# MLP units regrouped into ten blocks of 128 and one of 96 in a two-layer decode step

## The chip, the cores and the metric

The kernel runs on one core of a Trainium2 chip. The metric is the device time of one execution in microseconds; a version's time is the median over its runs. The engines that matter here are TensorE (PE, with its weight loads shown apart as PEld), VectorE (DVE), ScalarE (ACT), GpSimd (POOL), and SyncE (SP), whose queue issues every data transfer. The transfers run on 16 DMA engines.

## What is computed

One token (a row x of 512 numbers) passes through attention A, MLP B, attention A, MLP B, each with a layer norm before it and a residual sum after it. Both layers use the same weights and the same cache.

```python
# A: 32 heads of 128, cache of 4096 keys
q = layernorm(x) @ wq                       # 512 -> 32 x 128
p = softmax((q . k_cache) * 128 ** -0.5)    # per head, over 4096 keys
x = x + (p . v_cache) @ wo                  # 32 x 128 -> 512
# B: 1376 units
h = gelu(layernorm(x) @ w1 + b1)            # 512 -> 1376
x = x + h @ w2 + b2                         # 1376 -> 512
```

Everything is 32-bit floating point. The key and value caches hold 32 x 4096 x 128 numbers each, so that a layer reads far more than it computes.

## The kernel before

The heads are taken in eight groups of four (`G`); layer 0 goes through the groups upwards and layer 1 downwards, so that the last group's caches, and part of the group before it, need not be read twice. For each group `scores` (L230) multiplies the query with the keys, `softmax` follows, and the values are summed either on TensorE (`values`, L260) or on VectorE and ScalarE (`weighted`, L271, `weighted_by_act`, L265). All weights and caches come into one large tile, `arena`, by transfers that `load` (L85) issues on SP's queue in an order written out by hand. A transfer that overwrites a place waits on SP's queue for the last reader of that place, and all later transfers queue behind it.

The MLP (`mlp`, L335) has 1376 hidden units. Before the change they are split in four runs of `FJ` = 344 units, one for each quadrant of 32 partitions, and each run is cut into eleven pieces (`FB`) of 32. Block c, the c-th piece of each of the four runs, so holds 4 x 32 = 128 units, except that the last piece of each run has only 24. The host fills the last block of w2 with zero rows, so that w2 is 128 partitions x 11 x 512 numbers, 256 KB for each block.

`hidden(i)` (L349) computes the units of the blocks in `HIDDEN[i]`, (0 to 3), (4 to 7), (8 to 10), with four products side by side for each quarter of the input, each for one quadrant of 32 output partitions: 128 columns each, and 88 each for the last three blocks. `turned(i)` (L364) transposes the result on VectorE, `gelu` (L370) applies the scale, bias and activation, and the loop from L409 multiplies each block's 128 values with the 128 partitions of its piece of w2 (L414), four products for a block, one for each quarter of the 512 outputs. In the profile each of those 32-bit products shows as two records. All 44 products add into `pM`.

`W2_PARTS` (L47) cuts the transfers of w2: blocks 0-3, 4-5, 6-7, 8-9 and 10 in layer 0, and 0-3, 4-7, 8-9 and 10 in layer 1. Block 10 is a transfer of its own in both layers. In layer 0 there is room for eight blocks (`W2_AT`), so the transfers of blocks 8-9 and of block 10 are issued, through `follow` (L622), after the products of block 3; block 10 goes where block 2 was. In layer 1 they are the last two transfers into the core, and the products of blocks 8 to 10, a sum at L640 and the store of the output at L641 end the kernel.

Of the kernel before, what the change touches and what calls it, by code (L numbers as in the profile page):

```python
# [17 lines left out]
P = 128  # L18
D = 512
H, S, DH = 32, 4096, 128  # L20
F = 1376
G = 8
J = 4
C = 8
FJ = F // J
FB = 11
EPS = 1e-5
U = 512
KEPT = 6

NC = 4 * U
# [3 lines left out]
SPARE = 2 * BLOCK + STAY  # L35
# [4 lines left out]
AHEAD = 64  # L40
X_AT, B1_AT, B2_AT = 0, 8, 8 + FB
K2_HOME = 12 * NC

V1_HOME = *(2 * BLOCK + NC * c for c in range(5)), 8 * NC, 6 * NC, 7 * NC
W2_AT = tuple(SPARE + U * (c % 8) for c in range(FB)), tuple(U * c for c in range(FB))
PITCH = 1024
W2_PARTS = ((0, 4), (4, 6), (6, 8), (8, 10), (10, FB)), ((0, 4), (4, 8), (8, 10), (10, FB))  # L47
HIDDEN = ((0, 4), (4, 8), (8, FB))
W1_AT = (0, 4 * J * 32 * 4, 4 * J * 32 * 8)
# [11 lines left out]
def decode_layers(ctx: ExitStack, tc: tile.TileContext, k, v, w, w1, w2, out):  # L61
    nc = tc.nc
# [20 lines left out]
    arena = const.tile([P, ARENA], F32, name="arena")  # L83

    def load(at, src):  # L85
        t = arena[:, at : at + src.shape[-1]]
        tc.keep_in_program_order(nc.sync.dma_start(t, src))  # L87
        return t

    def pin(ins):  # L90
        tc.keep_in_program_order(ins)

    def chunk(t, i=0):
        return t[:, NC * i : NC * (i + 1)].rearrange("p (j n) -> p j n", j=4)
# [31 lines left out]

    fixed = small("fixed", 2 * FB + 7)
    b1c, colsum, b2c = fixed[:, :FB], fixed[:, FB : 2 * FB], fixed[:, 2 * FB : 2 * FB + 4]
# [20 lines left out]
    pM, pN = pO[:, 2 * P : 3 * P], pO[:, 3 * P :]  # L149
# [185 lines left out]
    def mlp(xs, s, w1_t, w2_t, xb, rows, fill, follow):  # L335
        hs, rstd = pH[layer], []
        if fill is None:
            nm, ss, _ = mean_of(xs, s, pN[:, 0:1], True)
            nm_s, nmr, cb, late = small("nm_s"), small("negm"), colsum, HIDDEN[0][1]
            nc.vector.tensor_copy(nm_s, nm)  # L340
        else:
            centred = small("xs", 8).rearrange("p (c i) -> p c i", i=2)
            nc.gpsimd.memset(centred[:, :, 1], 1.0)
            _, ss, _ = mean_of(xs, s, pN[:, 0:1], True, centred[:, :, 0])
        nc.gpsimd.tensor_tensor(xb, xs[:, :, 0], b2c, op=ALU.add)
        if fill is not None:
            xs = centred

        def hidden(i):  # L349
            at, first = hs[i], W1_AT[i]  # L350
            n = min(32 * HIDDEN[i][1], FJ) - 32 * HIDDEN[i][0]
            for c in range(4):
                for j in range(J):
                    f = first + n * (J * c + j)
                    pin(nc.tensor.matmul(at[32 * j : 32 * j + 2, :n], xs[:, c, :], w1_t[:, f : f + n],
                                         start=(c == 0), stop=(c == 3)))
                if i == 0 and c == VAR_AT:
                    rstd.append(rstd_of(ss, pN[:, 1:2], True))
                if i == 0 and c == VAR_AT and fill is None:
                    nc.gpsimd.tensor_tensor(nmr, nm_s, rstd[0], op=ALU.mult)  # L360
                    nc.gpsimd.tensor_scalar(cb[:, late:], colsum[:, late:], nmr, None, op0=ALU.mult)
                    nc.gpsimd.tensor_tensor(cb[:, late:], cb[:, late:], b1c[:, late:], op=ALU.add)

        def turned(i):  # L364
            ht = work.tile([P, 32 * 4], F32, name="pt")
            n = HIDDEN[i][1] - HIDDEN[i][0]
            pin(nc.vector.transpose(ht[:, : 32 * n], hs[i][:, : 32 * n]))  # L367
            return ht

        def gelu(i, ht):  # L370
            b0, b1_ = HIDDEN[i]
            n = b1_ - b0
            h, u, g = (small("gelu_" + k, FB)[:, b0:b1_] for k in "hug")
            if fill is not None:
                pin(nc.vector.scalar_tensor_tensor(u, of_32(ht, n), rstd[0], b1c[:, b0:b1_], op0=ALU.mult, op1=ALU.add))  # L375
                nc.gpsimd.tensor_copy(colsum[:, b0:b1_], of_32(ht, n, 1))
            elif i > 0:
                pin(nc.vector.scalar_tensor_tensor(u, of_32(ht, n), rstd[0], cb[:, b0:b1_], op0=ALU.mult, op1=ALU.add))
            else:
                pin(nc.vector.scalar_tensor_tensor(h, of_32(ht, n, 1), nm_s, of_32(ht, n), op0=ALU.mult, op1=ALU.add))  # L380
                pin(nc.vector.scalar_tensor_tensor(u, h, rstd[0], b1c[:, b0:b1_], op0=ALU.mult, op1=ALU.add))
            nc.scalar.activation(g, u, AF.Gelu_apprx_tanh)  # L382
            if fill is not None and b1_ == FB:
                nc.scalar.activation(small("m"), g[:, :1], AF.Exp, scale=0.0)
            return g

        if fill is not None:
            idle(fill, pS, 2 * P)
        hidden(0)
        if fill is None:  # L390
            hidden(1)
            pin(nc.vector.transpose(rows[:, P : 2 * P], rows[:, :P]))
        ht = turned(0)
        if fill is None:
            hidden(2)
        else:
            idle(fill, pO, 2 * P)
            idle(fill, pO, 2 * P)
        for i, (b0, b1_) in enumerate(HIDDEN):
            if i == 1 and fill is not None:  # L400
                for n in (512, 256):
                    idle(fill, pS, n)
                hidden(1)
                ht = turned(1)
                idle(fill, pS, 2 * P)
            g = gelu(i, ht)
            if fill is None and b1_ < FB:
                ht = turned(i + 1)
            for c in range(b0, b1_):  # L409
                if c == b0 + 2 and i == 1 and fill is not None:  # L410
                    hidden(2)
                    ht = turned(2)
                for j in range(J):
                    pin(nc.tensor.matmul(pM[32 * j : 32 * j + 1, :], g[:, c - b0 : c - b0 + 1],  # L414
                                         w2_t[c][:, P * j : P * (j + 1)], start=(c == 0), stop=(c == FB - 1)))
                for at, src in follow.get(c, ()):
                    load(at, src)
            if i == 1 and fill is not None:
                idle(fill, pS, 2 * P)
# [15 lines left out]
    w2_t = [[arena[:, at : at + U] for at in homes] for homes in W2_AT]  # L435
# [4 lines left out]
    for layer in range(2):  # L440
# [23 lines left out]
        for n, g in enumerate(order):  # L464
            first, final = n == 0, n == G - 1
# [55 lines left out]
            elif final:  # L521
# [9 lines left out]
                for a, b in END_PARTS[layer]:  # L531
                    at = BLOCK - NC + U * a
# [20 lines left out]
            if layer == 1 and n == 0:  # L553
                wo_t = chunk(arena[:, PAIR : PAIR + NC])
            elif final:
                at = PAIR + NC * layer
                for a, b in WO_PARTS[layer]:
                    load(at + U * a, of_w(wo_at(g), 1)[:, U * a : U * b])
                wo_t = chunk(arena[:, at : at + NC])
                if layer == 0:  # L560
                    load(HELD, w1[:, : W1_AT[1]])
                for a, b in W2_PARTS[layer][: 1 if layer == 0 else 4]:
                    load(W2_AT[layer][a], w2[:, U * a : U * b])
                if layer == 0:
                    load(HELD + W1_AT[1], w1[:, W1_AT[1] : W1_AT[2]])
            else:
                t = load(PAIR, of_w(wo_at(g) if layer == 0 else wq_at(g - 1), 2))
                wo_t, wq_next = (chunk(t, i) for i in ((0, 1) if layer == 0 else (1, 0)))
# [17 lines left out]
            if final:  # L586
                if layer == 0:
                    row_to_quadrants(row)
                    for a, b in W2_PARTS[0][1:3]:
                        load(W2_AT[0][a], w2[:, U * a : U * b])  # L590
                        if a == 4:
                            load(HELD + W1_AT[2], w1[:, W1_AT[2] :])
                idle(last_v, pO, 256)
# [15 lines left out]
        at = work.tile([P, P], F32, name="pt")  # L609
# [9 lines left out]
        if layer == 0:  # L619
            first_k, next_wq = part(k, G - 2, 0, 1), of_w(wq_at(G - 2), 1)  # L620
            follow = {
                3: (*((W2_AT[0][a], w2[:, U * a : U * b]) for a, b in W2_PARTS[0][3:]),  # L622
                    (SPARE + NC - U, first_k[:, NC - U :])),
                5: ((SPARE + NC, next_wq[:, : 2 * U]),),
                7: ((SPARE + NC + 2 * U, next_wq[:, 2 * U :]),),
                9: ((SPARE, first_k[:, : 2 * U]),),
            }
        mlp(x1, s1, w1_t, w2_t[layer], xb, *((None, last_v) if layer == 0 else (ends, None)), follow)
        if layer == 0:
# [4 lines left out]
            g = G - 2  # L634
# [9 lines left out]
def columns(a):  # L644

    return np.ascontiguousarray(a.reshape(J, 4, 32, -1).transpose(0, 2, 1, 3).reshape(P, 4, -1))
# [41 lines left out]
```

## Time and profile before

| | us |
|---|---|
| median of the three runs | 675.82 |
| the three runs | 673.79, 675.82, 676.31 |
| the profiled execution | 673.33 |
| span in its profile (first to last instruction) | 671.6 |
| around the span | 1.7 |

The profile is of one execution. Its span is what the views below divide up; the 1.7 us around it belong to the execution's time and to no instruction. Times in the views are counted from the span's start. A transfer "lands" when its last part is there; the name on the right of an arrow is what is read, on the left what is written.

### The profile page before, as it was taken

How to read it: one execution, taken by the hardware profiler on the slowest of the kernel's cores; microseconds unless marked ns; L12 is line 12 of the kernel's file. 1: busy time of each engine (PE TensorE's matmuls, PEld its weight loads, DVE VectorE, ACT ScalarE, POOL GpSimd, SP SyncE). 2: the span in 40 equal slices, each digit the busy share in tenths (PEclk: the TensorE clock that was granted, in tenths of full speed). 3: DMA queues.
4: the chain of work that ended last, by engine and by line, in shares of the span. 5: the costliest groups of instructions: out<-in, count | busy, mean ns of one | idle time of the engine just before them, and what ended most of it. 6: DMA issues, size and time to landing. Idle time of an engine off the chain costs nothing.

```text
span 671.6 us, 6013 instructions
## 1 busy us (share of the span) xinstructions
PE 299.7 (45%) x2236; PEld 79.7 (12%) x2236; DVE 407.1 (61%) x510; ACT 215.4 (32%) x697; POOL 5.2 (1%) x26
## 2 busy tenths in 40 slices
PE   1511703415116053165768986704316025065597
PEld 1000100101001010011114311101001001011124
DVE  3059679498696886971322313288597694973513
ACT  0047074190560823802011200083290650910010
POOL 1000000000000000000000000000000000000000
PEclk9965755757558557578689998655757559557799
DMA  9999999999999999999999999999999999999997
GB/s 377 437 437 438 435 437 437 403 461 437 437 437 397 444 426 434 433 429 426 425 415 399 422 422 438 437 433 433 431 433 437 437 430 402 462 426 414 431 414 286
DMA packets 11556, 285.29 MB, mean 425 GB/s; under 512 B 1284, under 2 KB 1288, under 8 KB 3720
## 3 DMA queue, kind: packets, MB, share of 16 engines
q1 hardware_dynamic: 11528, 284.92, 99.1%
q8 instruction: 17, 0.28, 0.2%
q14 instruction: 11, 0.09, 0.0%
HBM read 284.92 MB, written 0.00 MB: 424 GB/s over the span
## 4 chain that ended last, share of the span: by engine, by line
DMA 64%; PE 17%; DVE 15%; issue 1%; another core or an unknown queue 1%; SPq 1%; ACT 0%; DVEq 0%; ACTq 0%
DMA arena<-in_v 37%; DMA arena<-in_k 24%; PE pS L232 8%; DVE arena L274 7%; PE pO L262 5%; DMA arena<-in_w 4%; DVE arena L279 3%; DVE arena L311 2%; PE pO L283 1%; DVE arena L287 1%; DVE arena L215 1%; SPq L87 1%; PE pB L323 1%; DVE arena L309 0%
## 5 line engine op out<-in xcount | busy, mean ns | idle before, releaser
L269 ACT ACTIVATE arena<-arena,pt 128x128 f32<-128x128 f32 x640 | 188.0, 387 | 50.8 <-DMA arena<-in_v 48.1
L232 PE MATMUL pS<-arena,smalls 128*8 128x512 f32 x1024 | 147.0, 727 | 78.4 <-DMA arena<-in_k 74.3
L279 DVE TENSOR_TENSOR arena<-arena 128x4096 f32<-128x4096 f32 x30 | 132.6, 4420 | 0.3
L274 DVE TENSOR_TENSOR arena<-arena,pt 128x2048 f32<-128x2048 f32 x40 | 89.0, 2287 | 36.8 <-DMA arena<-in_v 35.7
L217 PE MATMUL pS<-arena,smalls 128*128 128x512 f32 x20 | 20.7, 1140 | 202.5 <-DVE arena L215 202.5
L244 ACT ACTIVATE arena<-pS,smalls 128x512 f32<-128x512 f32 x16 | 12.4, 777 | 289.4 <-DVE smalls L243 289.4
L287 DVE STREAM_TRANSPOSE arena<-pO 128x512 f32<-128x512 f32 x16 | 11.5, 717 | 97.4 <-PE pO L262 61.9
L262 PE MATMUL pO<-arena,pt 128*4 128x512 f32 x368 | 48.9, 666 | 11.8 <-DMA arena<-in_v 11.0
L232 PEld LDWEIGHTS pS<-arena,smalls 128*8 128x8 f32 x1024 | 29.8, 102 | 198.6 <-issue 177.3
L236 DVE TENSOR_REDUCE smalls<-pS 128x1 f32<-128x512 f32 x16 | 11.0, 687 | 64.1 <-PE pS L232 64.1
L215 DVE SCALAR_TENSOR_TENSOR arena<-arena,smalls 128x512 f32<-128x512 f32 x45 | 33.8, 752 | 1.6
L311 DVE SCALAR_TENSOR_TENSOR arena<-arena,smalls 128x512 f32<-128x512 f32 x39 | 29.3, 752 | 1.4
L217 PEld LDWEIGHTS pS<-arena,smalls 128*128 128x128 f32 x20 | 5.0, 311 | 206.2 <-DVE arena L215 206.2
L315 PE MATMUL pB<-arena,smalls 128*1 128x512 f32 x26 | 14.7, 648 | 29.0 <-DVE arena L311 29.0
L246 PE MATMUL pO<-ident,arena 128*128 128x128 f32 x64 | 13.4, 344 | 28.1 <-ACT arena L244 27.8
L574 DVE TENSOR_TENSOR arena<-arena 128x2048 f32<-128x2048 f32 x10 | 22.9, 2292 | 0.3
L382 ACT ACTIVATE smalls<-smalls 128x4 f32<-128x4 f32 (+1 forms) x6 | 1.2, 205 | 44.0 <-DVE smalls L375 25.6
L262 PEld LDWEIGHTS pO<-arena,pt 128*4 128x4 f32 x368 | 9.8, 93 | 44.8 <-issue 42.4
L250 DVE STREAM_TRANSPOSE smalls<-smalls 128x32 f32<-128x32 f32 x16 | 3.4, 212 | 17.5 <-ACT arena L244 17.5
L246 PEld LDWEIGHTS pO<-ident,arena 128*128 128x128 f32 x64 | 8.4, 167 | 42.1 <-ACT arena L244 36.7
L244 ACT ACT_TABLE_LOAD x1 | 1.3, 1283 | 36.9 <-DVE smalls L243 36.9
L438 PE MATMUL pS<-arena,ident 128*8 128x256 f32 (+1 forms) x34 | 11.9, 454 | 0.5 <-DVE pt L367 0.5
(115 smaller groups left out, 183.6 us busy)
## 6 DMA issues: line engine op xcount, KB each, us to landing
arena<-in_w SPq DMA_DIRECT2D x13, 2048.0 KB, 12.5
arena<-in_k SPq DMA_DIRECT2D x6, 4096.0 KB, 21.3
arena<-in_v SPq DMA_DIRECT2D x2, 4096.0 KB, 25.1
arena<-in_w SPq DMA_DIRECT2D x6, 1024.0 KB, 30.9
arena<-in_v SPq DMA_DIRECT2D x2, 2048.0 KB, 37.0
arena<-in_k SPq DMA_DIRECT2D x2, 2048.0 KB, 13.4
arena<-in_w SPq DMA_DIRECT2D x7, 512.0 KB, 9.3
arena<-in_v SPq DMA_DIRECT2D x3, 1024.0 KB, 46.3
```

The costliest lines, as they stand in the source:

```text
L215: pin(nc.vector.scalar_tensor_tensor(t, wt[:, c, :], xc[:, c : c + 1], t, op0=ALU.mult, op1=ALU.add))
L217: pin(nc.tensor.matmul(at, one.to_broadcast([P, P]), t, start=True, stop=True))
L232: pin(nc.tensor.matmul(pS[32 * j : 32 * j + C, :], z[:, j, C - 1 - c : 2 * C - 1 - c], kt[:, j, :], start=(c == 0), stop=(c == C - 1)))
L246: nc.tensor.transpose(pT[:, b].rearrange("p j r -> p (j r)"), p[:, P * b : P * (b + 1)], ident)
L262: nc.tensor.matmul(pO[32 * j : 32 * j + 4, :], pt[:, j, c, :], by_head(vt)[:, j], start=(i == 0), stop=(i == of - 1))
L269: nc.scalar.activation(own, own, AF.Copy, scale=pt[:, j, c, b : b + 1])
L274: nc.vector.tensor_tensor(own, own, weight, op=ALU.mult)
L279: pin(nc.vector.tensor_tensor(a, a, b, op=ALU.add))
L287: nc.vector.transpose(ot[:, :512], pO)
L311: pin(nc.vector.scalar_tensor_tensor(t, wt[:, d, :], on[:, d : d + 1], t, op0=ALU.mult, op1=ALU.add))
L315: pin(nc.tensor.matmul(pB[0:1, :], one, t, start=n == 0, stop=n == G - 2))
L574: pin(nc.vector.tensor_tensor(total, total, other, op=ALU.add))
```

## The change

The units are regrouped: block c now holds the units 128 c to 128 c + 127, and the last block the 96 units that are left. The zero rows of w2 that were spread over the last block's four quadrants (8 in each) become the 32 partitions 96 to 127. `load_w2` transfers block 10 over 96 partitions (`FULL`) and the other blocks over 128. The four products of block 10 contract over 96 rows. In `hidden`, the last group of blocks has 96, 96, 96 and 64 columns for the four quadrants in place of 88 each. The transfers of blocks 8-9 and 10 in layer 0 are issued by `load_w2` at the same point, after the products of block 3 and ahead of the key transfer that `follow` still issues there. The host's layouts of w1, w2 and b1 follow; their sizes in memory are unchanged.

```diff
+FULL = F - P * (FB - 1)
...
+    def load_w2(layer, a, b):
+        at, rows = W2_AT[layer][a], FULL if b == FB else P
+        pin(nc.sync.dma_start(arena[:rows, at : at + U * (b - a)], w2[:rows, U * a : U * b]))
...
-            n = min(32 * HIDDEN[i][1], FJ) - 32 * HIDDEN[i][0]
+            b0, b1_ = HIDDEN[i]
+            ns = [32 * (b1_ - b0 - (b1_ == FB and j == J - 1)) for j in range(J)]
             for c in range(4):
-                for j in range(J):
-                    f = first + n * (J * c + j)
+                for j, n in enumerate(ns):
+                    f = first + sum(ns) * c + sum(ns[:j])
...
+                used = FULL if c == FB - 1 else P
...
-                    pin(nc.tensor.matmul(pM[32 * j : 32 * j + 1, :], g[:, c - b0 : c - b0 + 1],
-                                         w2_t[c][:, P * j : P * (j + 1)], start=(c == 0), stop=(c == FB - 1)))
+                    pin(nc.tensor.matmul(pM[32 * j : 32 * j + 1, :], g[:used, c - b0 : c - b0 + 1],
+                                         w2_t[c][:used, P * j : P * (j + 1)], start=(c == 0), stop=(c == FB - 1)))
+                if layer == 0 and c == 3:
+                    for a, b in W2_PARTS[0][3:]:
+                        load_w2(0, a, b)
...
-                    load(W2_AT[layer][a], w2[:, U * a : U * b])
+                    load_w2(layer, a, b)
...
-                        load(W2_AT[0][a], w2[:, U * a : U * b])
+                        load_w2(0, a, b)
...
-                3: (*((W2_AT[0][a], w2[:, U * a : U * b]) for a, b in W2_PARTS[0][3:]),
-                    (SPARE + NC - U, first_k[:, NC - U :])),
+                3: ((SPARE + NC - U, first_k[:, NC - U :]),),
```

## Rows read from the trace of the kernel before

**Rows 1.** The page: busy time, slices, and bytes of all transfers.

```profile
span 671.6 us, 6013 instructions
...
PE 299.7 (45%) x2236; PEld 79.7 (12%) x2236; DVE 407.1 (61%) x510; ACT 215.4 (32%) x697; POOL 5.2 (1%) x26
...
DMA  9999999999999999999999999999999999999997
GB/s 377 437 437 438 435 437 437 403 461 437 437 437 397 444 426 434 433 429 426 425 415 399 422 422 438 437 433 433 431 433 437 437 430 402 462 426 414 431 414 286
DMA packets 11556, 285.29 MB, mean 425 GB/s; under 512 B 1284, under 2 KB 1288, under 8 KB 3720
```

**Rows 2.** Windows: counts and busy us by engine, clock, DMA share, GB/s.

```profile
300.00:340.00 40.00, 23.49 (x142) 4.97 (x142) 14.07 (x37) 6.02 (x11) 0.00 (x0) 0.83 0.99 426
...
354.00:366.00 12.00, 10.33 (x200) 5.44 (x194) 2.31 (x12) 0.41 (x2) 1.23 (x5) 1.00 1.02 412
366.00:370.00 4.00, 3.09 (x76) 1.81 (x80) 0.99 (x5) 1.69 (x3) 0.19 (x1) 1.00 0.97 347
370.00:414.00 44.00, 38.43 (x304) 10.12 (x295) 10.36 (x40) 4.97 (x10) 0.55 (x1) 0.96 1.01 423
...
656.00:664.00 8.00, 6.99 (x122) 3.49 (x124) 2.98 (x14) 0.00 (x0) 0.28 (x2) 1.00 1.03 412
```

**Rows 3.** The chain that ended last, around both MLPs: start, us, what.

```profile
359.50 0.68 PE pO L414 x17
360.18 7.25 DMA arena<-in_w
367.43 0.14 issue
367.57 1.00 PE pO L414 x24
...
414.61 24.39 DMA arena<-in_v
...
624.34 31.69 DMA arena<-in_v
656.04 11.41 DMA arena<-in_w
667.46 0.14 issue
667.59 1.00 PE pO L414 x24
668.62 0.29 DVE arena L640
```

**Rows 4.** Windows of the last 4 us of the transfers, columns as in Rows 2.

```profile
664.00:664.50 0.50, 0.50 (x29) 0.48 (x22) 0.31 (x2) 0.00 (x0) 0.47 (x1) 1.00 0.94 385
...
665.50:666.00 0.50, 0.50 (x32) 0.47 (x25) 0.39 (x2) 0.21 (x1) 0.00 (x0) 1.00 0.70 279
666.00:666.50 0.50, 0.50 (x28) 0.38 (x20) 0.32 (x2) 0.11 (x1) 0.00 (x0) 1.00 0.66 258
666.50:667.00 0.50, 0.50 (x28) 0.48 (x24) 0.00 (x0) 0.10 (x1) 0.00 (x0) 1.00 0.46 176
667.00:667.50 0.50, 0.37 (x16) 0.08 (x4) 0.00 (x0) 0.00 (x0) 0.00 (x0) 1.00 0.34 111
667.50:668.00 0.50, 0.41 (x16) 0.34 (x16) 0.00 (x0) 0.00 (x0) 0.00 (x0) 1.00 0.02 8
```

**Rows 5.** Timeline, end of layer 0's MLP: start, us, engine, line [idle before].

```profile
364.93 0.79 PE L355 MATMUL pS<-arena,smalls 128*2 128x88 f32 x32 [0.35 <-DMA arena<-in_w]
...
366.42 0.21 ACT L382 ACTIVATE smalls<-smalls 128x3 f32<-128x3 f32 x1 [2.51 <-DVE smalls L375]
...
367.57 0.96 PE L414 MATMUL pO<-arena,smalls 128*1 128x128 f32 x24 [0.33 <-DMA arena<-in_w]
...
368.13 0.10 PEld L414 LDWEIGHTS pO<-arena,smalls 128*1 128x1 f32 x8 [0.24 <-DMA arena<-in_w]
```

**Rows 6.** Timeline, end of layer 1's MLP, columns as in Rows 5.

```profile
663.94 1.06 PE L355 MATMUL pB<-arena,smalls 128*2 128x128 f32 x32
...
665.42 1.95 PE L414 MATMUL pO<-arena,smalls 128*1 128x128 f32 x64
...
666.39 0.20 ACT L382 ACTIVATE smalls<-smalls 128x3 f32<-128x3 f32 x1 [0.44 <-DVE smalls L378]
667.56 0.35 PEld L414 LDWEIGHTS pO<-arena,smalls 128*1 128x1 f32 x16 [0.48 <-issue]
...
668.15 0.11 PEld L414 LDWEIGHTS pO<-arena,smalls 128*1 128x1 f32 x8 [0.23 <-DMA arena<-in_w]
```

**Rows 7.** Line L414: durations in ns (min/median/max) and forms.

```profile
L414 PE MATMUL pO<-arena,smalls x176: 269/272/273, 359.5 to 668.3; 128*1 128x128 f32 x176
```

**Rows 8.** Transfer issues by size: line or tile, count, KB, us to landing.

```profile
arena<-in_w SPq DMA_DIRECT2D x4, 256.0 KB, 16.5
...
out<-arena SPq DMA_DIRECT2D x1, 2.0 KB
```

More of the change, by code (lines that the diff above doesn't have):

```diff
@@ L651 @@
         x=A_x, k=A_k_cache, v=A_v_cache, wq=A_wq, wo=A_wo, w1=B_w1, b1=B_b1, w2=B_w2, b2=B_b2).items()}
-    pad = 32 * FB - FJ
-    w2 = np.pad(a["w2"].reshape(J, FJ, D), ((0, 0), (0, pad), (0, 0)))
-    b1 = np.pad(a["b1"].reshape(J, FJ), ((0, 0), (0, pad)))
-    w1 = columns(a["w1"]).reshape(P, 4, J, FJ)
+    w2 = np.pad(a["w2"], ((0, P * FB - F), (0, 0))).reshape(FB, P, D)
+    b1 = np.pad(a["b1"], (0, P * FB - F)).reshape(FB, P)
+    w1 = columns(a["w1"])
     wq = columns(a["wq"]).reshape(P, 4, G, J, J, 32)
@@ L663 @@
         (X_AT, columns(a["x"])[:, :, 0]),
-        (B1_AT, b1.reshape(J, FB, 32).transpose(0, 2, 1).reshape(P, FB)),
+        (B1_AT, b1.T),
         (B2_AT, columns(a["b2"])[:, :, 0]),
@@ L671 @@
         w=w,
-        w1=np.concatenate([w1[..., 32 * a : 32 * b].reshape(P, -1) for a, b in HIDDEN], axis=1),
-        w2=w2.reshape(J, FB, 32, D).transpose(0, 2, 1, 3).reshape(P, FB * D),
+        w1=np.concatenate([w1[:, c, f : f + 32] for a, b in HIDDEN for c in range(4) for j in range(J)
+                           for f in range(P * a + 32 * j, min(P * b, F), P)], axis=1),
+        w2=w2.transpose(1, 0, 2).reshape(P, FB * D),
     )
```

## The prediction

> **What bounds the kernel now.** I read the page first. No compute engine is near its limit: VectorE is busy for 61% of the span and TensorE for 45%, while the row of the DMA engines shows a 9 in 39 of the 40 slices, with 437 GB/s in its plain stretches [rows 1]. So I read the chain of waits next, to see which transfers set the end, and at which places compute steps in between them. Around the two MLPs the reader is to see the same pattern twice. In layer 0 the products of L414 start at 359.50, run out of data, and wait 7.25 us for w2; then 1.00 us of products closes the layer. In layer 1 the chain is a value transfer of 31.69 us, w2's 11.41 us, the same 1.00 us of products, one sum, and the output [rows 3]. Both times the thing that is late is w2, and its last piece is block 10, which the change makes smaller.
>
> The windows say what such a transfer waits for. From 300 us to 664 us the DMA share stays between 0.97 and 1.03 in each of the windows shown, so w2 is not slow by itself; it stands in a queue that is always full [rows 2]. A microsecond saved in the queue in layer 0 therefore isn't lost in a pause before the end. The last windows show one thing more: the DMA share doesn't stop at once but falls over two microseconds, 0.70, 0.66, 0.46, 0.34, 0.02 between 665.5 and 668 us [rows 4]. The 16 engines finish their parts at different times, and the products wait for the last one. What counts at the end is thus how much the slowest engine has to move, not the mean.
>
> The timeline shows how far block 10 is from being the bound. The products of blocks 8 and 9 begin at 367.57 us in layer 0 and at 667.59 us in layer 1 [rows 3]; the weight loads of block 10 follow at 368.13 and 668.15, after an idle 0.24 and 0.23 us for the transfer [rows 5, 6]. In both layers block 10 is still awaited after the products of 8 and 9 were issued.
>
> **The change part by part.** *The transfer of block 10.* It is 128 rows of 512 numbers of 4 bytes, 262,144 bytes (the page's 256 KB) [rows 8]; at the queue's 437 GB/s [rows 1] that is 0.60 us. Over 96 rows it is 196,608 bytes, or 0.45 us, if the rows are spread evenly over the 16 engines (6 rows for each, where it had 8). That saves 0.15 us in each layer, 0.30 us together: 131,072 bytes of 285.29 MB, 0.05%. Layer 0's saving reaches the end because the queue is never empty behind it [rows 2]; layer 1's because the last engine's share shrinks, and it is within the idle 0.23 us before block 10 [rows 6].
>
> No load of the trace runs over 96 partitions; all have 128 but the output's 4 rows [rows 8], so the price has to be bounded. From below: if the slowest engine is one that has 4 of the 96 rows left, it saves twice as much, 0.30 us in layer 0, and in layer 1 the 0.23 us that the wait is long, 0.53 us together. From above: if the rows aren't spread further than over half of the engines, each of those has 12 rows in place of 8 and takes half as long again, +0.30 us a layer, +0.60 us in all. I take the even spread, because it is what the 128-row loads at full rate are nearest to.
>
> [...]
>
> *The products of block 10.* Contracting over 96 rows leaves four products for the block, each 128 columns wide, and a record at L414 takes 269 to 273 ns, all 176 of them over 128 rows [rows 7]. I take no difference. The bound: were each one cut in two for its rows, 8 records would become 16; 64 records take 1.95 us [rows 6], about 0.03 us each, so 8 more cost 0.24 us a layer, 0.48 us in all. A gain has no reason: the same records with the same columns.
>
> *The hidden products.* The last three blocks have 96, 96, 96 and 64 columns in place of four times 88, the same 352 in sum. 32 records with 88 columns take 0.79 us and 32 with 128 columns 1.06 us [rows 5, 6], so 40 columns cost 0.27 us, and if the widest quadrant sets the pace, 8 more cost 0.05 us; if the sum does, nothing. That is hidden. In layer 0 their activation is done at 366.63, and the first product that needs it starts at 367.57, when w2 lands: 0.9 us of cover [rows 5]. In layer 1 the activation ends at 666.59, and TensorE is done with the earlier 64 records at 667.37, 0.2 us before it is released by w2 [rows 6, 3]. Were the cover gone, the cost would be the 0.05 us in each layer. The transposes, biases and activations keep their sizes.
>
> *The order of transfers.* In layer 0 the two last loads of w2 move from the loop over `follow` to a line just ahead of it, at the same block, before the same key transfer; their number, waits and place on SP's queue are unchanged. Block 10 still goes over block 2's place, whose products are in order ahead of it, and the next user of that place still waits for block 10's products. Cost nothing, and nothing moves behind it: the queues of the other engines issue no transfers.
>
> **The sum.** 673.33 us, the profiled execution's own time, less 0.30 us: 673.03 us. That execution is below the three other runs (673.79, 675.82, 676.31), and which of these levels a run takes isn't decided by 0.3 us. The middle of the four is 674.8 us, and less 0.3 us I forecast 674.5 us.
>
> **The rivals.** *The load isn't shorter.* If half of the engines keep 8 rows each and the others get 4, and the last one to finish is of the first half, block 10 lands when it did; the gain is 0 and the time 674.8 us. For it: the windows show that the last engine decides [rows 4], and it needn't be one that is relieved. Against it: only that an even split is as natural. *The load gets longer, slower side.* The place is block 10's transfer in both layers; the mechanism is that 96 rows are dealt to few engines. With n engines, each moves 96/n rows where it had 8, and a row costs an engine 0.60/8 = 0.075 us. With one engine that is 7.2 us in place of 0.6, +6.6 us a layer, +13.2 us and 688.0 us in all. It decides (3.4 us in all, 1.7 us a layer) once an engine has 31 rows, with three engines or fewer. For it: nothing in the trace excludes it, since no large load is short of 128 rows. Against it: 96 divides by 16 as 128 does. *The products of 96 rows are slower*: cut in two, by the bound above, +0.48 us less the 0.30 gained, 675.0 us. *A gain worth seeing*: it would need 3.4 us, and both of w2's block 10 transfers together hold the queue for only 1.2 us. I see no place for it in the rows.
>
> **How the numbers follow.** About 0.5% (3.4 us) is what a measurement of this kernel can tell from no change; the three runs of before alone lie 2.5 us apart. Chances: even spread 0.52; no shorter load 0.33; slower products or half of the engines 0.06; few engines 0.05; something that I don't see and that makes it faster 0.04. The first three are all within 0.5%, so same has 0.91, slower 0.05, faster 0.04. The likeliest time is 674.5 us. The range is set by where a median of these runs can fall, and by the bounds: down to 673.33 less 0.53, 672.8 us, and up to 676.31 plus 0.60, 676.9 us.
>
> **What would show it.** In the profile after, the gap between the landing of blocks 8-9 and of block 10, seen as the time between the last two groups of weight loads at L414 (0.59 us in both layers [rows 5, 6]), should shrink to about 0.45 us; if it stays, the load isn't shorter. The total should be 0.13 MB less. The records at L414 should stay 176 of about 272 ns; more records or longer ones show the products wrong. A landing of block 10 several microseconds after that of blocks 8-9 would show few engines, and the forecast wrong. The fall of the DMA share over the last 2 us should look as before.

## The result and the profile after

| | before | after |
|---|---|---|
| median of 22 runs each, us | 673.91 | 675.25 |
| lowest to highest, us | 673.13 to 676.31 | 674.65 to 676.37 |
| span of the profiled execution, us | 671.6 | 672.9 |

The ratio is 1.0016 with a 95% interval of 1.0009 to 1.0023: the change costs 1.1 us (0.16% of 673.9). (The ratio and its interval come from all runs of both kernels; the quotient of the two medians is 1.0020.) That is inside "within 0.5%" and inside the forecast range, but it has the wrong sign: the forecast was a gain of 0.30 us. With 22 runs a side, a difference that three runs could not have told apart stands clear of noise.

The page of the changed kernel first. Its columns are those of [rows 1]:

```profile
span 672.9 us, 6013 instructions
...
GB/s 376 436 436 437 438 432 436 410 456 436 432 436 406 464 437 414 432 421 424 434 410 380 401 428 446 436 432 429 427 432 436 432 429 410 464 433 407 429 416 278
DMA packets 11492, 285.16 MB, mean 424 GB/s; under 512 B 1284, under 2 KB 1288, under 8 KB 3656
```

The bytes fell as forecast, by 0.13 MB; 64 packets of the 2 KB kind are gone, 32 in each layer. So the load does what the diff says, and still the span is 1.3 us longer. The chain that ended last says at which places (start, us, what; to be read against [rows 3]):

```profile
359.37 1.10 PE pO L421 x32
360.46 8.44 DMA arena<-in_w
368.95 0.44 PE pO L421 x8
...
415.39 23.69 DMA arena<-in_v
...
656.96 11.98 DMA arena<-in_w
668.95 0.14 issue
669.08 0.88 PE pO L421 x24
669.99 0.29 DVE arena L649
```

In layer 0 the last group of products now starts at 368.95, where block 10's weight loads stood at 368.13 [rows 5]: 0.82 us later, though the first products began 0.13 us earlier. A lag of this size, 0.92 us, is there when the wait for w2 in layer 1 starts, 656.96 against 656.04 [rows 3]. Whether it is the same lag can't be read from two executions; the experiments below say more. Layer 1's wait is 11.98 us instead of 11.41 and adds another 0.57 us; the products after it take 0.12 us less because all three blocks are there at once, and the last sum starts 1.37 us later than before (669.99 against 668.62). In these two profiles the loss sits in the two stretches of the chain that w2 holds, here called its waits.

The windows tell what happened in the first of them. Columns as in [rows 2]:

```profile
354.00:366.00 12.00, 10.29 (x196) 5.47 (x194) 2.40 (x12) 0.41 (x2) 1.24 (x5) 1.00 1.01 399
366.00:370.00 4.00, 2.46 (x44) 1.12 (x44) 0.74 (x4) 1.69 (x3) 0.19 (x1) 1.00 1.00 320
370.00:414.00 44.00, 38.30 (x320) 10.50 (x324) 10.51 (x41) 4.96 (x10) 0.55 (x1) 0.96 1.00 416
```

The DMA engines are as busy as before (1.01, 1.00, 1.00), but they move less: 399 GB/s where [rows 2] had 412, 320 where it had 347, 416 where it had 423. Busy without moving bytes is what a row of DMA share hides: an engine counts as busy for as long as its packet takes. The queue's own row for 363 to 369 us, around the landing of blocks 8 to 10 in layer 0 (packets, MB, share of the 16 engines), shows it most plainly. Before:

```profile
q1 hardware_dynamic: 740, 2.23, 99.9%
```

After:

```profile
q1 hardware_dynamic: 657, 1.96, 100.1%
```

12% fewer bytes in the same 6 us, with engines equally busy. Packets must have become longer, and block 10's load moves only 0.20 MB in all. The timeline of the changed kernel (columns as in [rows 5]) shows that the load ahead of it is hit too:

```profile
364.78 0.83 PE L361 MATMUL pS<-arena,smalls 128*2 128x96 f32 x32 [0.35 <-DMA arena<-in_w]
...
366.62 0.62 PE L421 MATMUL pO<-arena,smalls 128*1 128x128 f32 x16 [1.01 <-DMA arena<-in_w]
...
368.17 0.35 PEld L421 LDWEIGHTS pO<-arena,smalls 128*1 128x1 f32 x16 [1.02 <-ACT smalls L390]
368.20 1.15 PE L421 MATMUL pO<-arena,smalls 128*1 128x128 f32 x24 [0.55 <-DMA arena<-in_w]
...
368.95 0.11 PEld L421 LDWEIGHTS pO<-arena,smalls 96*1 96x1 f32 x8 [0.43 <-DMA arena<-in_w]
...
669.05 0.57 PEld L421 LDWEIGHTS pO<-arena,smalls 128*1 128x1 f32 x24 [1.02 <-issue]
```

The products of blocks 8 and 9 start at 368.20, not 367.57 as in [rows 5], though their load was issued before block 10's, over 128 partitions as ever, and nothing of it was changed. The weight loads of block 10 follow theirs after 0.78 us (368.17 to 368.95), not the 0.59 us of before or the 0.45 us of the forecast. Blocks 6 and 7, whose load was issued earlier still, are late already: their products start at 366.62, and in the kernel before at 366.21:

```profile
366.21 0.62 PE L414 MATMUL pO<-arena,smalls 128*1 128x128 f32 x16 [0.49 <-DMA arena<-in_w]
```

In layer 1 the weight loads of all three blocks come in one group of 24 at 669.05: block 10 is no longer awaited after blocks 8 and 9.

### The profile page after: what moved, and what is told of

It reads as the page before. It is cut to its first block, busy times and chain, and to the rows that moved or that the text cites. A ratio compares the mean times of both kernels' runs of the same rounds, so it can differ in the third digit from the quotient of the medians.

```text
span 672.9 us, 6013 instructions
## 1 busy us (share of the span) xinstructions
PE 297.5 (44%) x2236; PEld 79.9 (12%) x2236; DVE 407.0 (60%) x510; ACT 215.4 (32%) x697; POOL 5.2 (1%) x26
## 2 busy tenths in 40 slices
DMA packets 11492, 285.16 MB, mean 424 GB/s; under 512 B 1284, under 2 KB 1288, under 8 KB 3656
## 4 chain that ended last, share of the span: by engine, by line
DMA 64%; PE 17%; DVE 15%; issue 1%; another core or an unknown queue 1%; SPq 1%; ACT 0%; DVEq 0%; ACTq 0%
DMA arena<-in_v 37%; DMA arena<-in_k 24%; PE pS L237 8%; DVE arena L279 7%; PE pO L267 5%; DMA arena<-in_w 4%; DVE arena L284 3%; DVE arena L316 2%; PE pO L288 1%; DVE arena L292 1%; DVE arena L220 1%; SPq L88 1%; PE pB L328 1%; DVE arena L314 0%
## 5 line engine op out<-in xcount | busy, mean ns | idle before, releaser
L237 PE MATMUL pS<-arena,smalls 128*8 128x512 f32 x1024 | 144.1, 715 | 78.1 <-DMA arena<-in_k 73.9
L267 PE MATMUL pO<-arena,pt 128*4 128x512 f32 x368 | 51.9, 682 | 10.9 <-DMA arena<-in_v 10.1
## 6 DMA issues: line engine op xcount, KB each, us to landing
arena<-in_w SPq DMA_DIRECT2D x13, 2048.0 KB, 12.8
```

What stands on the lines that cost most here:

```text
L237: pin(nc.tensor.matmul(pS[32 * j : 32 * j + C, :], z[:, j, C - 1 - c : 2 * C - 1 - c], kt[:, j, :], start=(c == 0), stop=(c == C - 1)))
L267: nc.tensor.matmul(pO[32 * j : 32 * j + 4, :], pt[:, j, c, :], by_head(vt)[:, j], start=(i == 0), stop=(i == of - 1))
```

## Experiments

Eleven kernels were run, in three sets; each set was timed against runs of the kernel before on the same chip. The medians of before were 673.24, 673.43 and 673.35 us in 29, 33 and 15 runs; each experiment has 4 to 11 runs. The ratios in the tables come from all runs, as above, and differ from quotients of medians by up to 0.07%.

### Which part of the change costs the time

`load128` undoes the short load alone, and `before_load96` makes it alone.

```diff
 load128, in the changed kernel's load_w2:
-        at, rows = W2_AT[layer][a], FULL if b == FB else P
+        at, rows = W2_AT[layer][a], P
 before_load96, in the kernel before:
...
-                    load(W2_AT[layer][a], w2[:, U * a : U * b])
+                    rows = 96 if b == FB else P
+                    load(W2_AT[layer][a], w2[:rows, U * a : U * b], rows)
...
+                3: ((W2_AT[0][8], w2[:, U * 8 : U * 10]), (W2_AT[0][10], w2[:96, U * 10 :], 96),
```

> The changed kernel with block 10 of w2 loaded over all 128 partitions again; its products still contract over 96 rows and the units stay regrouped. Theory A (the 96-partition loads disturb the DMA engines): the time is that of the kernel before, ratio 1.000 within 0.001, and the weight loads of block 10 follow those of blocks 8 and 9 after 0.6 us in layer 0 again. Theory B (the 96-row products or the uneven hidden columns cost the time, the load doesn't): the ratio stays near 1.0016.

> The kernel before with one part of the change alone: block 10 of w2 is loaded over its first 96 partitions in both layers; units, hidden products and the 128-row products stay as they were (so 24 of the last units meet numbers that stood there earlier: the output isn't the reference's). Theory A: the whole loss of the change, ratio 1.0013 to 1.002. Theory B: ratio 1.000 or 0.3 us under it, 0.9995.

| | median, us | ratio to before | 95% interval |
|---|---|---|---|
| `load128` | 673.43 | 1.0002 | 0.9993 to 1.0011 |
| `before_load96` | 674.89 | 1.0027 | 1.0016 to 1.0037 |

With the 128-partition load the loss is gone, although the units are regrouped, the hidden products uneven and the products 96 rows deep. With the 96-partition load alone it is there. Theory B falls: the load alone brings a loss of at least this size. The 1.0027 lies above Theory A's 1.0013 to 1.002; its interval and that of the change (1.0009 to 1.0023) overlap.

`only_layer0` and `only_layer1` keep the short load in one layer.

```diff
-        at, rows = W2_AT[layer][a], FULL if b == FB else P
+        at, rows = W2_AT[layer][a], FULL if b == FB and layer == 0 else P   # only_layer1: layer == 1
```

> The changed kernel with the 96-partition load in layer 0 alone; layer 1 loads block 10 over 128 partitions. Theory A, with what the two profiles show at each place: 0.8 to 0.95 us of the loss is made in layer 0, so ratio 1.0012 to 1.0014, and w2's last wait in layer 1 is as long as before. Theory C (only the very end of the kernel counts, since the queue makes up for what is lost in layer 0): ratio 1.000.

> The changed kernel with the 96-partition load in layer 1 alone. Theory A: 0.4 to 0.5 us, ratio 1.0006 to 1.0008, and layer 0's last product ends where it did before. Theory C: the whole loss, ratio 1.0016.

| | median, us | ratio to before | 95% interval |
|---|---|---|---|
| `only_layer0` | 674.30 | 1.0021 | 1.0012 to 1.0031 |
| `only_layer1` | 673.77 | 1.0011 | 1.0003 to 1.0020 |

Both layers pay. The chain of `only_layer0` has the late last products in layer 0 and, in layer 1, the wait for w2 that the kernel before has (11.41 us in [rows 3]):

```profile
360.68 8.15 DMA arena<-in_w
368.87 0.44 PE pO L421 x8
...
656.90 11.43 DMA arena<-in_w
668.33 0.14 issue
668.47 1.00 PE pO L421 x24
```

In the chain of `only_layer1` layer 0 isn't late (367.30 against 367.57), and the wait in layer 1 is longer:

```profile
360.04 7.13 DMA arena<-in_w
...
367.30 1.01 PE pO L421 x24
...
657.33 12.66 DMA arena<-in_w
```

This execution took 675.21 us, the longest of its eleven. It starts the wait 1.29 us later than the profile of before, though layer 0 lost nothing. `load128`, which has no short load at all, starts it late too:

```profile
656.88 11.39 DMA arena<-in_w
668.27 0.14 issue
668.41 1.00 PE pO L421 x24
```

So where this wait starts differs by 0.84 and 1.29 us between these executions and that of before, and a profile alone doesn't show that layer 0's loss lasts to the end. The times do: Theory C, that the queue makes up for what is lost in layer 0, falls with the interval of `only_layer0`. The two ratios come out above what Theory A took from the profiles (1.0012 to 1.0014 and 1.0006 to 1.0008), but the intervals reach down to these. Together they are twice the loss of the change, so how it divides between the layers stays open.

### What about 96 partitions is costly

Four kernels differ from the changed one only in how block 10 is loaded.

```diff
 load_w2, block 10 in two loads (t = arena, at = its columns, n = 512):
+ two_halves128:  t[:, at : at + n//2], t[:, at + n//2 : at + n]
+ contig_64_32:   t[0:64, at : at + n], t[64:96, at : at + n]
+ stepped_64_32:  t[0:128:2, at : at + n], t[1:128:4, at : at + n]
 load_w2, block 10 in one load:
+ rows_112:       t[0:112, at : at + n]
```

> Control for the number of loads: the changed kernel with block 10 loaded as two loads of all 128 partitions, 256 columns each (the bytes of the kernel before). If one more load costs nothing by itself: ratio 1.000 within 0.0007. If a load more is what hurts: 1.001 or above.

> The changed kernel with block 10 loaded as partitions 0 to 63 and partitions 64 to 95, two loads, the same 96 rows. Theory P (a load of all 128 partitions gives every DMA engine its own group of partitions, evenly over the whole range; a load of another range sends several engines to the same part of the memory, and their packets wait for each other): the rows lie at the low end even more, so at least the loss of the single 96-partition load, ratio 1.002 to 1.005. Theory R (only a number of rows for each engine like 6 hurts; 4 and 2 don't): 0.9995 to 1.000.

> As the load in two pieces of 64 and 32 rows, but spread over the whole range: partitions 0, 2, 4, ..., 126 and then 1, 5, 9, ..., 125 (rows that the products don't read are loaded and some that they read aren't, so the output isn't the reference's). The same bytes, rows and loads. Theory P: each part of the memory gets its even share, the packets keep their length, ratio 0.9995 to 1.0005. A theory by which any load over other than 128 partitions hurts: 1.002 or above, as with the two pieces side by side.

> The changed kernel with block 10 loaded over 112 partitions (7 rows for each of 16 engines; the last 16 are zeros that nothing reads). Theory P: between 96 and 128, ratio 1.0005 to 1.002. Theory that it is the missing quadrant of 32 partitions alone that counts, in proportion: half of the loss, 1.001. Theory that any count but 128 hurts alike: 1.0016 to 1.0027.

| | rows | loads | median, us | ratio to before | 95% interval |
|---|---|---|---|---|---|
| `two_halves128` | 128 | 2 | 673.42 | 1.0001 | 0.9992 to 1.0010 |
| `contig_64_32` | 96 | 2 | 674.99 | 1.0018 | 1.0009 to 1.0027 |
| `stepped_64_32` | 96 | 2 | 673.43 | 1.0000 | 0.9991 to 1.0009 |
| `rows_112` | 112 | 1 | 674.60 | 1.0013 | 1.0004 to 1.0022 |

The second and third row are the test. The same number of rows, bytes and loads; only the places differ, and the loss goes from 0.18% to none. (Theory P had put `contig_64_32` at 1.002 or more; 1.0018 is just under.) So it isn't a price for a load of fewer than 128 partitions, nor for a number of rows that isn't a power of two, nor for one more load; it is where the rows lie. Each of these loads reads the same rows of w2 as it writes partitions, so whether the places written or the places read count is not separated by any run. Theory R had 0.9995 to 1.000 for `contig_64_32` and falls. The queue's row for the same 363 to 369 us agrees. `contig_64_32`:

```profile
q1 hardware_dynamic: 672, 1.96, 99.2%
```

`stepped_64_32`:

```profile
q1 hardware_dynamic: 745, 2.22, 96.3%
```

The one is like the changed kernel, the other like the one before. The packets themselves, from the trace's records of them, all 2 KB packets that start in the 9 to 10 us from 361 us on:

```
                 median ns   longest ns
before                     85         96
after                     118        189
contig_64_32              110        251
rows_112                  125        168
stepped_64_32              85         98
```

The other loads pay as well. The 4 KB packets that start from 365 to 368 us belong to loads that no edit touched, blocks 8 and 9 among them: their median is 162 ns before and in `stepped_64_32`, and 189 in the changed kernel, 189 in `contig_64_32` and 206 in `rows_112`.

`rows_112` leaves only 16 partitions out and loses 0.13%. Its interval holds half of the changed kernel's loss and all of it, so it doesn't decide whether the loss goes with what is missing; its packets are no shorter than those of the changed kernel.

The two places in ten profiles: the start of VectorE's first step behind layer 0's last products (L632 before the change), and the length of the last wait for w2.

| | layer 0, us | last wait, us |
|---|---|---|
| before | 368.65 | 11.41 |
| `load128` | 368.67 | 11.39 |
| `two_halves128` | 368.57 | 11.42 |
| `stepped_64_32` | 368.37 | 11.39 |
| `only_layer0` | 369.39 | 11.43 |
| `only_layer1` | 368.39 | 12.66 |
| after | 369.47 | 11.98 |
| `before_load96` | 369.34 | 12.08 |
| `rows_112` | 369.38 | 11.99 |
| `contig_64_32` | 369.51 | 12.80 |

Wherever a short load over neighbouring partitions stands, layer 0 ends at 369.3 to 369.5 instead of 368.4 to 368.7, and the last wait takes 12.0 to 12.8 us instead of 11.4. Nothing falls in between.

### More and fewer bytes, evenly and unevenly

The last three enlarge the load in question. They load blocks 8 to 10 in the same two loads as the changed kernel: half of the partitions, evenly or not, or all the rows in an uneven cut.

```diff
 load_w2:
+ half_stepped:    rows 0:128:2 for blocks 8-9 and for block 10
+ half_contig:     rows 0:64    for blocks 8-9 and for block 10
+ blocks8to10_96:  rows 0:96 of blocks 8-10 (6 KB a row), then rows 96:128 of blocks 8-9 (4 KB a row)
```

> The changed kernel with blocks 8 to 10 of w2 loaded over every second partition only (0, 2, ..., 126; half of their bytes are left out in both layers, so the output isn't the reference's). It asks whether fewer bytes pay when they are spread evenly. 393,216 bytes less in each layer at 437 GB/s: 0.90 us a layer, 1.8 us in all, ratio 0.9973. If only layer 1's saving counts: 0.9987. If bytes don't count here: 1.000.

> The same with partitions 0 to 63 in place of every second one: the same bytes left out, the same loads, the output isn't the reference's either. Theory P: the partitions that are left lie in one half of the range, the packets wait for each other, and the saved 1.8 us are lost again or more than lost: ratio 1.000 to 1.004. Against P: as with every second partition, 0.997.

> The suspected cost three times: the changed kernel with blocks 8 to 10 loaded as 96 partitions of 6 KB rows and then blocks 8 and 9 as the last 32 partitions of 4 KB rows; two loads as in the changed kernel, the same bytes, the same output. Theory P: the loss grows with the bytes that lie unevenly, up to three times, ratio 1.003 to 1.006. If the loss is a fixed price for each load of other than 128 partitions: two such loads for one, 1.003 to 1.0035 at most, and 1.0016 if the load of 32 is free.

| | bytes against before | median, us | ratio to before | 95% interval |
|---|---|---|---|---|
| `half_stepped` | -0.79 MB | 672.27 | 0.9985 | 0.9976 to 0.9994 |
| `half_contig` | -0.79 MB | 676.45 | 1.0053 | 1.0041 to 1.0066 |
| `blocks8to10_96` | -0.13 MB | 682.52 | 1.0137 | 1.0120 to 1.0154 |

With the same bytes left out, every second partition gains 1.0 us and the lower 64 partitions lose 3.6 us. Fewer bytes do pay here, but not when they are missing from one half. The loss is above the 1.000 to 1.004 that Theory P had. The gain is smaller than the 1.8 us of the estimate; the chain of `half_stepped` shows why at the end:

```profile
664.01 0.65 PE pS L361 x23
664.66 2.45 PE pO L421 x85
...
667.14 0.29 DVE arena L649
```

w2 is no longer waited for in layer 1 at all: TensorE goes through all its products without a stop, and a load that lands still earlier has nothing more to give there.

`blocks8to10_96` costs 9.2 us, above the 1.006 that Theory P allowed and the 1.0035 of a fixed price for each load. Its chain:

```profile
360.45 10.71 DMA arena<-in_w
371.30 1.46 PE pO L427 x24
...
663.74 12.83 DMA arena<-in_w
676.56 0.14 issue
676.70 1.50 PE pO L427 x24
```

Layer 0's last products start at 371.30, 3.7 us late against [rows 3]. And then the loss grows: the wait for w2 in layer 1 starts at 663.74, 7.7 us late. Part of it goes with what its windows show (columns as in [rows 2]):

```profile
366.00:370.00 4.00, 1.74 (x24) 0.59 (x18) 0.51 (x2) 1.69 (x3) 0.29 (x2) 0.78 1.02 213
370.00:374.00 4.00, 2.70 (x38) 1.37 (x42) 0.64 (x3) 0.00 (x0) 0.00 (x0) 0.50 0.83 269
374.00:414.00 40.00, 34.42 (x276) 9.81 (x272) 10.55 (x40) 4.96 (x10) 0.55 (x1) 0.93 0.99 409
```

TensorE had little to do in the long wait (1.74 of 4 us), and its granted clock went from 1.00 to means of 0.78 (366 to 370 us) and 0.50 (370 to 374 us), just when layer 1's first products were due. The 24 records at 371.30 took 1.46 us, for 1.00 in the kernel before [rows 3], at a granted clock of 1.00; the kernels before and after the change have 1.00 from 366 to 370 us and a mean of 0.96 from there to 414. How much of the 4 us between the two places comes from the clock, and what the rest is, was not tried.

## Why the prediction was wrong

**Right.** What bounds the kernel: both losses sit in the waits for w2 that [rows 3] showed, and by the time of `only_layer0` what is lost there in layer 0 reaches the end. (I called the 7.25 us a wait; they aren't idle time. From 354 to 366 us TensorE was busy for 10.33 of 12 us [rows 2], and its own idle time before the last products was 0.33 us [rows 5].) The products of 96 rows cost what those of 128 do; the changed kernel's line L421 still has 176 records of the same length:

```profile
L421 PE MATMUL pO<-arena,smalls x176: 269/272/274, 359.4 to 669.7; 128*1 128x128 f32 x160, 96*1 96x128 f32 x16
```

The hidden products of the last three blocks take 0.83 us for 0.79, as bounded (0.05), and hidden as forecast. The order of transfers cost nothing: `load128` has it too (1.0002). 0.13 MB less was moved. And that the change stays within 0.5% held.

**Wrong.** The step that failed is the price of block 10's transfer, -0.15 us a layer: "I take the even spread, because it is what the 128-row loads at full rate are nearest to". It multiplied rows by a fixed 0.075 us, as did the bound of +0.60 us, and it put the effect on other loads at nothing without a reason. The even spread that the 0.15 us rests on was my estimate, and no run shows it: the page's packets under 512 B are 1284 before and after, and from 360 to 369 us 111 after and 126 in `contig_64_32`, with its one more load, so they say nothing of the rows of each engine. What the runs showed in its place is that a packet's duration isn't a constant of its size. When a load's rows leave out the top of the partitions, 2 KB packets take 110 to 125 ns where they took 85, and the 4 KB packets of loads beside it 189 to 206 where they took 162. By the profiles that was worth +0.8 us at the end of layer 0 and +0.45 us in layer 1 (0.57 more of waiting, 0.12 less of products), where I had -0.15 each; by the times it was +1.1 us (0.6 to 1.6) where I had -0.30. Why the packets take longer stays open: that they wait for each other at one part of the memory, as Theory P has it, no run shows, and which engine wrote which partition is in no row.

That 675.25 us lies in the range, and only 0.75 us from the likeliest time, is luck. The base of 674.8 us, the middle of four executions, was 0.9 us above the median of 22 (673.91), which hides more than half of the error, and the range was drawn wide by the spread of single runs. Among the chances there was none for an unseen effect that makes the kernel slower.

**The rivals.** "The load isn't shorter" came nearest, with a half that keeps its rows, but its consequence was too mild: it let block 10 land when it did before, and didn't ask what happens to the loads beside it. "Half of the engines", at +0.60 us the upper bound, is below the measured 1.1 us (0.6 to 1.6). "Few engines" found no support: block 10 lands within a microsecond of blocks 8 and 9, not several behind them.

**What would be better.** None of the versions that compute the whole step is faster than the kernel before: `load128` and `two_halves128` equal it. Placing the 96 units on evenly spread partitions could save 0.13 MB without the loss, but `stepped_64_32`, which moves just that, measured 1.0000, so there is nothing to be seen there.

## What to carry to other kernels

In this kernel, where a full DMA queue sets the time (its packets took 99% of the 16 engines' span), zero rows that fill a load up to all 128 partitions were cheaper than a shorter load over neighbouring partitions (1.0002 in `load128`, 1.0016 in the changed kernel). If bytes are to be saved in such a place, try taking them evenly, as every second partition did here (0.9985, for 1.0053 with the lower 64), and not from the top of the range; fewer columns on all partitions were not tried. To see such a loss, read GB/s beside the DMA share: a share that stayed full (1.02 and 1.01 from 354 to 366 us) while GB/s fell (412 to 399) went with longer packets here (2 KB in 118 ns for 85), and the loads beside the odd one (4 KB packets in 189 ns for 162) have to be looked at too.

## What the runs showed of the hardware

- A 192 KB load over 96 partitions, once in each of two layers, cost 1.1 us against one of 256 KB over 128, and a load that was issued ahead of it landed later: the products of blocks 8 and 9 started 0.63 us later in layer 0 (368.20 against 367.57).
- The median length of a 2 KB packet was 85 ns with full or evenly spread loads and 110 to 125 ns with loads that leave out the top of the partitions; one took 251 ns.
- 112 of 128 partitions were not better than 96 by anything that the intervals tell apart (1.0013 and 1.0016).
- The uneven cut of three blocks cost 9.2 us for the bytes of the changed kernel, and TensorE's granted clock fell from 1.00 to means of 0.78 from 366 to 370 us, in the long wait for w2 (busy for 1.74 of 4 us), and 0.50 from 370 to 374 us; 24 records from 371.30 on took 1.46 us for 1.00.
